# Infini-attention and a routed FFN on one core: logit maxima over two heads, the causal mask added by TensorE, four projection jobs per unit, and one emitted order for every engine

## The chip, the cores and the metric

The kernel runs on one core of one Trainium2 chip. The metric is device time in microseconds (us) of one launch; lower is better. The time of a kernel is the median over its runs. Engines: TensorE (PE; PEld is its weight load), VectorE (DVE), ScalarE (ACT), GpSimd (POOL), and SyncE (SP), which here issues all DMAs.

## The reference, cut to what matters

One sequence of S = 2048 tokens, D = 640, 32 heads of 20 channels. Attention is causal within segments of L = 512 tokens; across segments there is a linear memory `M`, `z`. Beside it stands one SwiGLU FFN for the single token with the largest router score. A sigmoid gate mixes the two.

```python
for s in range(N):                                   # N = 4 segments
    qs, ks, vs = q[:, :, s], k[:, :, s], v[:, :, s]
    logits = jnp.einsum("bhqd,bhkd->bhqk", qs, ks) * scale + mask
    a_dot = jnp.einsum("bhqk,bhkd->bhqd", _softmax(logits), vs)
    pq = phi(qs)                                     # where(t > 0, t + 1, exp(t))
    a_mem = (pq @ M) / ((pq @ z)[..., None] + 1e-6)
    outs.append(g * a_mem + (1.0 - g) * a_dot)
    pk = phi(ks)
    M = M + jnp.einsum("bhld,bhle->bhde", pk, vs)
    z = z + jnp.einsum("bhld->bhd", pk)
a = outs @ wo
...
y = (silu(x_sel @ w_gate) * (x_sel @ w_up)) @ w_down * sigmoid(r_sel)   # one token
b = x + scatter(y)
return gate * a + (1 - gate) * b
```

## The kernel before

**Number format.** Products that must be exact to float32 are made of float32r parts: a tensor is split into `hi` (an ACT copy that rounds) and `lo` (a subtraction, on POOL or DVE; L144 to L146), and a product takes three matmuls, hi hi, lo hi, hi lo.

**Units and groups.** The heads are cut into two halves of 16, the sequence into four segments; a *unit* `u` (8 of them) is one half in one segment, and a *group* `n` (32 of them, four a unit) is four heads of a unit.

**Projections** (`projections`, L407; `pair_up`, L230). In each unit five T jobs make q and k with channels on partitions (tiles of 128 channels, `TILES`), and two V jobs make v with tokens on partitions. A job runs in two halves of the PE array at once (rows 0 to 63 and 64 to 127; a *pair* is one matmul in each), 15 pairs, a drain, and 15 pairs with the halves swapped ("swap"). All jobs write the one PSUM tile `sums` (two banks), so a job can start only after the one before has been copied out: `evac_t` (L278) copies a T tile by halves with ACT and DVE (L284, L285) into the `lo` tile, casts `hi`, makes `phi` (two ACT passes, then DVE L293), and at last POOL overwrites the copy with `lo` (L298). `hi` and `lo` rows go by DMA to DRAM stacks (`place`, L252) and come back (`bring_back`, L268) as `qs` and `ks`, five buffers of each, so that one matmul of 60 rows makes all three products of a logit.

**Logits.** `a_step` (L496) makes logits with queries on partitions into PSUM `a`, five steps a group. DVE adds the mask (a bf16 tile) and takes the maximum in one instruction, per head (L507); an accumulator read follows each. `m_split` and `m_rows` turn the negative maxima into two more rows of `qs` (by DMA, L528). `b_step` (L531) makes the logits again with keys on partitions (`bt`, L537), now with the maximum subtracted by those rows; ACT takes the exponential (L539), POOL zeroes what lies above the diagonal (L543).

**Values and memory.** `pv_step` (L549) sums over keys on PE into `pv`, with 32-column tiles, and copies it to `pvs` (L558); `norm` transposes and divides; `memory_read`, `memory_write` and `keys` are the linear memory. The group's rows go to DRAM (`otok`).

**FFN** (`ffn`, L709). Routing, ten steps up (two weights, five each), an activation, eight steps down; each step loads `wt` (two buffers) and later multiplies. A step that yields 2 is one that has to wait for something.

**Output** (`out_stage`, L749). For each of 16 tiles of 128 tokens: rows of `otok` are read, transposed, split, multiplied with `wo` (30 pairs of 320 columns into `sums`), and added (L799) to `xf`, the gated residual: `x` loaded (L724) into one of the four `raw` buffers, scaled by ACT (L727), mixed by DVE with the FFN's row (L728).

**What sets the order.** PE and SP run in the order in which the code emits; ACT, DVE and POOL are ordered by the tile framework's scheduler. The emitted order is a fixed table of events per group (`plan`, L882): fractions of a group at which the steps of `a`, `b`, the maxima's rows and `full` (PV, norm and other chores, L858) stand; before each event the projections are run to `LEAD` = 3.6 groups ahead of the logits (`proj.to`). Loads and splits are tied to jobs (`prefetch`, L359). The FFN starts at n = 13 and takes one waiting step in each `full`; at n = 28 the rest of it is emitted at once, and then the output stage is started:

```python
            if n == 13 and k == 0:
                side.append(Fill(ffn()))
            if n == 28 and k == 0:
                for f in side:
                    f.finish()
                extra.append(Fill(out_stage()))
```

Of the kernel before, what the change touches and what calls it, by code (L numbers as in the profile page):

```python
# [19 lines left out]
NH = 2  # L20
# [26 lines left out]
JOBS = ("T0", "T1", "T2", "T3", "T4", "V0", "V2")  # L47
LAST = {"T1": 0, "T2": 1, "T3": 2, "T4": 3}
# [7 lines left out]
def tile_infini_mod(  # L56
# [27 lines left out]
    ctx.enter_context(tc.manual_schedule(engines={mybir.EngineType.PE, mybir.EngineType.SP}))  # L84
# [6 lines left out]
    mask = one.tile([128, L], BF16, name="mask")  # L91
    nc.vector.memset(mask, 0.0)
    nc.vector.tensor_scalar(mask[:, L - 128:], jp, 0.0, NEG, op0=OP.is_gt, op1=OP.mult)
    junk = one.tile([128, L], BF16, name="junk")
# [38 lines left out]
    W, raws = {}, {}  # L133

    def raw_tile(key, *srcs):
        t = pool.tile([128, D], F32, tag="raw", bufs=4, name="raw")
        n = 0
        for src in srcs:
            w = src.shape[-1]
            nc.sync.dma_start(t[:, n:n + w], src)  # L140
            n += w
        raws[key] = t[:, :n]

    def split(hi, lo, raw, eng):  # L144
        nc.scalar.copy(hi, raw)
        eng.tensor_tensor(out=lo, in0=raw, in1=f32(hi), op=OP.subtract)  # L146
# [6 lines left out]
    def w_tile(key):  # L153
        shape, tag, bufs = ([128, KT, VC + 2], "wv", 1) if key[0] == "V" else ([128, D], "w", KT + 1)
# [5 lines left out]
    def load_t(hf, j):  # L160

        for kind, g in READY[j]:
            t = pool.tile([128, KT, 4, DH], F32, tag="raw", bufs=4, name="raw")
            nc.sync.dma_start(t.rearrange("p k j d -> p k (j d)"), columns(kind, hf, g, GC).rearrange("(k p) m -> p k m", p=128))
            raws[kind, hf, g] = t

    def split_t(hf, j, eng=None):

        for kind, g in READY[j]:
            t = raws.pop((kind, hf, g))  # L170
            for i, tl in enumerate(TILES):
                for r0, r1, kind_, g_, c0 in tl:
                    if (kind_, g_) != (kind, g):
                        continue
                    hi, lo = W.get(("T", hf, i)) or w_tile(("T", hf, i))
                    src = t[:, :, :, c0 // 4:(c0 + r1 - r0) // 4].rearrange("p k j d -> p k d j")
                    h_, l_ = (f32(w).rearrange("p (k m) -> p k m", k=KT)[:, :, r0:r1].rearrange("p k (d j) -> p k d j", j=4)
                              for w in (hi, lo))
                    split(h_.bitcast(F32R), l_.bitcast(F32R), src, eng or nc.gpsimd)


    VPARTS = ((0, 0, 3), (0, 3, 5), (1, 0, 3), (1, 3, 5))

    def load_v(hf, i):
        qt, k0, k1 = VPARTS[i]
        w = 2 * GC + (2 if hf == 0 and qt == 0 else 0)
        t = pool.tile([128, D], F32, tag="raw", bufs=4, name="raw")[:, :(k1 - k0) * w].rearrange("p (k m) -> p k m", m=w)
        nc.sync.dma_start(t, columns("v", hf, 2 * qt, w).rearrange("(k p) m -> p k m", p=128)[:, k0:k1])
        raws["V", hf, i] = t

    def split_v(hf, i, eng=None):
        raw = raws.pop(("V", hf, i))
        qt, k0, k1 = VPARTS[i]
        w = raw.shape[2]
        hi, lo = W.get(("V", hf)) or w_tile(("V", hf))
        c = slice(162 * qt, 162 * qt + w)
        split(hi[:, k0:k1, c], lo[:, k0:k1, c], raw, eng or nc.gpsimd)

    def load_w(key):
        raw_tile(key, wo[128 * key[1]:128 * key[1] + 128, :])  # L200

    def split_w(key, eng=None):
        raw = raws.pop(key)
        hi, lo = w_tile(key)
        split(hi, lo, raw, eng or nc.gpsimd)


    X = {}

    def load_x(u, k):  # L210
        s = u % SEG
        raw_tile(("x", u, k), xT[128 * k:128 * k + 128, L * s:L * s + L])

    def split_x(u, k, eng=None):
        hi = pool.tile([128, L], F32R, tag="xhi", bufs=KT + 2, name="xhi")
        lo = pool.tile([128, L], F32R, tag="xlo", bufs=KT + 2, name="xlo")
        split(hi, lo, raws.pop(("x", u, k)), eng or nc.gpsimd)
        X[u, k] = hi, lo

    COST_MM = 1.08 / 2.4  # L220
    om = {}
    groups = [0]
    current = [0]
    chunks = [0.0]
    visits = [0]
    clock = [0]

    sums = psum.tile([128, 2, 512], F32, name="sums")

    def pair_up(o0, f0, o1, f1, cost):  # L230


        n = 3 * KT

        def mm(o, f, i, r, phase):
            return nc.tensor.matmul(o, *f(i, r), start=phase == 0 and i == 0, stop=phase == 1 and i == n - 1)  # L236

        for i in range(n):
            mm(o0, f0, i, 0, 0)
            mm(o1, f1, i, 1, 0)  # L240
            yield cost
        yield "swap"
        nc.tensor.drain()
        for i in range(n):
            mm(o1, f1, i, 0, 1)
            mm(o0, f0, i, 1, 1)
            yield cost

    aim = [0.0, 0.0]
    TOL = 0.11  # L250

    def place(kind, m, c0, hi, lo, r0, n):  # L252

        d = stk[kind][m % NS]
        first, gap, low = {"q": (0, GC, 2 * GC), "k": (0, 2 * GC, GC)}[kind]
        src = f32(hi)[r0:r0 + n, :L]
        nc.sync.dma_start(bass.AP(tensor=d.tensor, offset=d.offset + (first + c0) * L, ap=[[L, n], [gap * L, 2], [1, L]]),
                          bass.AP(tensor=src.tensor, offset=src.offset, ap=[list(src.ap[0]), [0, 2], list(src.ap[1])]))

        def low_rows():  # L260
            nc.sync.dma_start(d[low + c0:low + c0 + n, :], f32(lo)[r0:r0 + n, :L])
            if c0 + n == GC:
                backs.append((kind, m))
        lows.append(low_rows)

    lows, backs = [], []

    def bring_back():  # L268
        while backs:
            kind, m = backs.pop(0)  # L270
            assert m - NS < current[0]
            d = stk[kind][m % NS]
            dst = f32((qs if kind == "q" else ks)[m % NS])
            for b in range(2):
                nc.sync.dma_start(dst[64 * b:64 * b + ST].rearrange("r p t -> r (p t)"),
                                  d.rearrange("(r b p) t -> r b (p t)", b=2, p=2)[:, b])

    def evac_t(u, j):  # L278
        s = u % SEG
        hi = pool.tile([128, D], F32R, tag="hi", bufs=2, name="hi")  # L280
        lo = pool.tile([128, D], F32R, tag="lo", bufs=2, name="lo")
        c = f32(lo)[:, :L]
        h = L // 2
        nc.scalar.copy(c[:, :h], sums[:, 0, :h])  # L284
        nc.vector.tensor_copy(c[:, h:], sums[:, 1, :h])  # L285
        nc.scalar.copy(hi[:, :L], c)
        for r0, r1, kind, g, c0 in TILES[j]:
            place(kind, 4 * u + g, c0, hi, lo, r0, r1 - r0)
        if s < SEG - 1 or j in QGROUP:
            e = pool.tile([128, L], F32, tag="phi", bufs=3, name="phi")  # L290
            nc.scalar.activation(e, c, AF.Relu, scale=-1.0)
            nc.scalar.activation(e, e, AF.Exp, scale=-1.0)
            nc.vector.scalar_tensor_tensor(out=e, in0=c, scalar=1.0, in1=e, op0=OP.add, op1=OP.max)  # L293
            if s < SEG - 1:
                turned.append((clock[0], lambda: keys(u, j, e)))
            if s > 0 and j in QGROUP:
                chores.append((clock[0], lambda: memory_read(u, QGROUP[j], e)))
        nc.gpsimd.tensor_tensor(out=lo[:, :L], in0=c, in1=f32(hi)[:, :L], op=OP.subtract)  # L298
# [3 lines left out]
    def keys(u, j, e):  # L302
        for r in range(2):
            parts = [t for t in TILES[j] if t[2] == "k" and t[0] // 64 == r]
            if parts:
                p = slice(64 * r, 64 * r + 64)
                tp = psum.tile([128, 4, 64], F32, tag="misc", bufs=2, name="ktp")
                for c in range(4):
                    nc.tensor.transpose(tp[:, c, :], e[p, 128 * c:128 * c + 128], identf[p, p])
                for r0, r1, kind, g, c0 in parts:  # L310
                    nc.scalar.copy(kk[:, g, :, c0:c0 + r1 - r0], tp[:, :, r0 - 64 * r:r1 - 64 * r])

    def memory_read(u, g, e):
        nm = psum.tile([128, 4, GW], F32, tag="misc", bufs=2, name="nm")
# [656 lines left out]
```

## Time and profile before

| what | value |
|---|---|
| time, median of 3 runs | 879.21 us (877.89 to 883.76) |
| the profiled execution | 877.44 us |
| its span | 875.7 us |
| mean granted clock of PE | 0.89 of full speed |

The views quoted below are of that one execution. In the lists by line, a row is: line, engine, operation, output and inputs by the program's names, shape, count, then the busy time in us and the mean ns of one, then the idle time of the engine before them and what ended it. In the lists in order of time, a row is start, length (us) and what ran. In the waits, a row is who waited for whom, the total in us, how often, and the longest. Lengths of single matmuls are latencies; the rate is read from the distance of starts.

### The profile page before, as it was taken

How to read it: one execution, taken by the hardware profiler on the slowest of the kernel's cores; microseconds unless marked ns; L12 is line 12 of the kernel's file. 1: busy time of each engine (PE TensorE's matmuls, PEld its weight loads, DVE VectorE, ACT ScalarE, POOL GpSimd, SP SyncE). 2: the span in 40 equal slices, each digit the busy share in tenths (PEclk: the TensorE clock that was granted, in tenths of full speed). 3: DMA queues.
4: the chain of work that ended last, by engine and by line, in shares of the span. 5: the costliest groups of instructions: out<-in, count | busy, mean ns of one | idle time of the engine just before them, and what ended most of it. 6: DMA issues, size and time to landing. Idle time of an engine off the chain costs nothing.

```text
span 875.7 us, 19037 instructions
## 1 busy us (share of the span) xinstructions
PE 678.4 (77%) x7316; PEld 532.7 (61%) x7316; DVE 448.3 (51%) x1498; ACT 365.6 (42%) x646; POOL 257.4 (29%) x329
## 2 busy tenths in 40 slices
PE   5667887887878778878888888888874767776777
PEld 4556766666665666667766766666640345664766
DVE  5175555566455655675665566555560355422232
ACT  5333554545355545555554445444530034241110
POOL 3322233333345445243223323343340011021000
PEclk9878999999899989999999999898895679788889
DMA  4762357155525552563467256735644324133431
GB/s 125 204 210 59 97 141 202 25 140 149 145 63 147 168 155 70 169 185 80 140 190 234 80 154 183 210 105 176 192 135 130 99 91 130 54 113 92 133 93 61
DMA packets 81458, 116.67 MB, mean 133 GB/s; under 512 B 36240, under 2 KB 41880, under 8 KB 81368
## 3 DMA queue, kind: packets, MB, share of 16 engines
q1 hardware_dynamic: 81368, 115.46, 45.7%
q8 instruction: 58, 0.95, 0.5%
q14 instruction: 32, 0.26, 0.1%
HBM read 72.94 MB, written 41.96 MB: 131 GB/s over the span
## 4 chain that ended last, share of the span: by engine, by line
PE 30%; DMA 13%; DVE 12%; ACT 6%; issue 4%; SPq 3%; POOL 1%; POOLq 0%; DVEq 0%; ACTq 0%
PE sums L236 14%; DVE junk L507 6%; PE pv L555 6%; DMA xf<-in_x_dram 4%; DMA wt<-in_wd_dram 3%; DMA out_dram<-xf 3%; PE a L503 2%; PE nm L316 2%; SPq L528 2%; PE otp L575 1%; PE bt L537 1%; PE ffn L694 1%; DVE xf L799 1%; ACT p L539 1%; DMA stkk<-lo 1%
## 5 line engine op out<-in xcount | busy, mean ns | idle before, releaser
L507 DVE CUSTOM_DVE_ANT_0 junk<-a,mask 128x384 bf16<-128x384 f32 (+3 forms) x512 | 249.9, 488 | 147.3 <-PE a L503 136.6
L539 ACT ACTIVATE p<-bt 128x1024 f32<-128x1024 f32 x160 | 163.9, 1024 | 145.3 <-PE bt L537 144.5
L543 POOL TENSOR_SCALAR_AFFINE_SELECT p<-p 128x512 f32<-128x512 f32 (+1 forms) x160 | 87.3, 547 | 280.8 <-ACT p L539 271.6
L236 PE MATMUL sums<-xhi,whi 64*128 64x256 f32 x800 | 132.9, 325 | 41.5 <-DVE lo L285 26.1
L236 PE MATMUL sums<-xlo,whi 64*128 64x256 f32 x800 | 126.1, 306 | 1.2 <-POOL xlo L146 1.0
L236 PE MATMUL sums<-xhi,wlo 64*128 64x256 f32 x800 | 124.1, 303 | 0.0
L236 PEld LDWEIGHTS sums<-xhi,whi 64*128 64x128 f32 x800 | 85.6, 206 | 58.4 <-DVE lo L285 31.5
L503 PE MATMUL a<-ks,qs 60*128 60x384 f32 (+3 forms) x512 | 76.0, 347 | 45.9 <-DVE mx L507 42.0
L555 PE MATMUL pv<-p,va 128*32 128x512 f32 (+3 forms) x1024 | 84.0, 472 | 11.8 <-ACT num L318 9.9
L236 PEld LDWEIGHTS sums<-xlo,whi 64*128 64x128 f32 x800 | 86.6, 207 | 7.0 <-issue 3.7
L236 PEld LDWEIGHTS sums<-xhi,wlo 64*128 64x128 f32 x800 | 86.5, 208 | 0.5 <-issue 0.2
L503 PEld LDWEIGHTS a<-ks,qs 60*128 60x128 f32 x512 | 48.2, 203 | 57.4 <-DVE mx L507 52.3
L298 POOL TENSOR_TENSOR lo<-lo,hi 128x512 fp32r<-128x512 f32 x40 | 51.0, 1274 | 108.3 <-DVE phi L293 80.6
L236 PE MATMUL sums<-whi,oh 64*128 64x320 f32 x320 | 59.7, 361 | 29.3 <-DVE xf L799 26.7
L537 PE MATMUL bt<-qs,ks 62*128 62x384 f32 (+3 forms) x512 | 75.1, 344 | 7.7 <-ACT p L539 6.1
L236 PE MATMUL sums<-whi,xhi 64*128 64x322 f32 (+1 forms) x320 | 61.1, 369 | 13.4 <-DVE rg L352 5.5
L555 PEld LDWEIGHTS pv<-p,va 128*32 128x32 f32 x1024 | 33.9, 117 | 58.8 <-issue 37.4
L558 ACT COPY pvs<-pv 128x512 f32<-128x512 f32 x32 | 18.8, 586 | 103.6 <-PE pv L555 103.6
L236 PEld LDWEIGHTS sums<-whi,oh 64*128 64x128 f32 x320 | 35.9, 211 | 37.0 <-issue 24.3
L236 PE MATMUL sums<-whi,xlo 64*128 64x322 f32 (+1 forms) x320 | 58.0, 348 | 0.0
L537 PEld LDWEIGHTS bt<-qs,ks 62*128 62x128 f32 x512 | 49.1, 209 | 14.1 <-ACT p L539 10.8
L236 PE MATMUL sums<-wlo,xhi 64*128 64x322 f32 (+1 forms) x320 | 57.1, 343 | 0.0
(109 smaller groups left out, 1090.9 us busy)
## 6 DMA issues: line engine op xcount, KB each, us to landing
qs<-stkq SPq DMA_DIRECT2D x64, 240.0 KB
ks<-stkk SPq DMA_DIRECT2D x64, 240.0 KB
raw<-in_xT_dram SPq DMA_DIRECT2D x40, 256.0 KB
stkq<-hi SPq DMA_DIRECT2D x32, 320.0 KB
stkq<-lo SPq DMA_DIRECT2D x32, 160.0 KB
otok<-ou SPq DMA_DIRECT2D x32, 160.0 KB
xf<-in_x_dram SPq DMA_DIRECT2D x16, 320.0 KB
out_dram<-xf SPq DMA_DIRECT2D x16, 320.0 KB
```

What stands on the lines that cost most here:

```text
L236: return nc.tensor.matmul(o, *f(i, r), start=phase == 0 and i == 0, stop=phase == 1 and i == n - 1)
L298: nc.gpsimd.tensor_tensor(out=lo[:, :L], in0=c, in1=f32(hi)[:, :L], op=OP.subtract)
L316: nc.tensor.matmul(nm[:, c, :], e[:GC, 128 * c:128 * c + 128], mbd[:, g, :], start=True, stop=True)
L503: nc.tensor.matmul(a[:, b, at:at + w], q_, ks[n % NS][64 * b:64 * b + ST, p, :w], start=True, stop=True)
L507: nc.vector.tensor_tensor_reduce(out=junk[:, :w], in0=a[:, b, at:at + w], in1=mask[:, L - w:], scale=1.0, scalar=-3e38, op0=OP.add, op1=OP ...
L528: nc.sync.dma_start(f32(qs[n % NS])[64 * b + ST + r:64 * b + ST + r + 1].rearrange("r p (i t) -> r (p i) t", t=128), mr[16 * b + 8 * r:16 ...
L537: nc.tensor.matmul(bt[:, b, at:at + w], k_, qs[n % NS][64 * b:64 * b + ST + 2, p, L - w:], start=True, stop=True)
L539: nc.scalar.activation(pt, bt, AF.Exp, scale=SCALE)
L543: nc.gpsimd.affine_select(out=d, in_=d, pattern=[[0, e[1]] for e in dims[:-1]] + [[1, 128]], base=0, channel_multiplier=-1, compare_op=OP. ...
L555: nc.tensor.matmul(pv[32 * j:32 * j + 32, 128 * c:], va[u % 2][:, c, VW * h:VW * h + 32], pt_tiles[n, j % 2, c][:, j // 2], start=c == 0, ...
L558: nc.scalar.copy(pvs[n], pv)
L575: nc.tensor.transpose(tp[:, c].rearrange("p j r -> p (j r)"), o[:, 128 * c:128 * c + 128], identf)
```

## The change

Five things are done at once.

1. *Maxima.* One `tensor_reduce` takes the maxima of both heads of a step (two PSUM banks) in place of one masked maximum and one accumulator read per head.
2. *Mask on PE.* After each logit row, four more matmuls (two heads of 64 rows times two halves of the array; 128 columns) add the mask's diagonal block into PSUM: `pick` (a shifted identity) times `tri` (-1e30 above the diagonal).
3. *Four jobs per unit.* Two T jobs make two whole tiles each (512 columns in each bank); the fifth tile is cut into 128-column parts that run ahead of the V part in the other two jobs.
4. *Order by a rough clock.* `now` holds a time for each engine; every emitted piece adds an estimated duration and is marked with when its result, its PSUM buffer or its DMA will be there. The main loop emits a logit step, PV, a chore or a projection pair when that clock says it is ready. Loads stand in one list and are issued when a `raw` buffer is free; DMAs are issued when the clock passes the time of their data. `LEAD` is 3.9. FFN steps that wait run at any visit; the output stage follows the projections in the same stream, `x` is loaded two tiles at a time into the buffers of the V weights, and the mix is done one tile ahead.
5. *Emitted order on all engines:* ACT, DVE and POOL too.

Beside these, the copy of a T tile now lies in `phi` (so POOL's `lo` reads it, and DVE's `phi` step overwrites it after that), the `w` ring has one buffer less, and the fifth tile is evacuated and placed in two halves.

```diff
-    LEAD = 3.6
+LEAD = 3.9
-    ctx.enter_context(tc.manual_schedule(engines={mybir.EngineType.PE, mybir.EngineType.SP}))
+    ctx.enter_context(tc.manual_schedule())
...
+    for h in range(2):
+        for r in range(2):
+            p = slice(64 * r, 64 * r + 64)
+            off = 64.0 * (h - r)
+            nc.vector.tensor_scalar(pick[p, h], jp[p], off, None, op0=OP.is_equal)
+            nc.vector.tensor_scalar(tri[p, h], jp[p], off, NEG, op0=OP.is_gt, op1=OP.mult)
...
     def a_step(n, k):
...
         for i, p, at, w in LOGITS[k]:
             for b in range(2):
                 q_ = qs[n % NS][64 * b:64 * b + ST, p, 128 * i:128 * i + 128]
-                nc.tensor.matmul(a[:, b, at:at + w], q_, ks[n % NS][64 * b:64 * b + ST, p, :w], start=True, stop=True)
+                nc.tensor.matmul(a[:, b, at:at + w], q_, ks[n % NS][64 * b:64 * b + ST, p, :w], start=True, stop=False)
+            for h in range(2):
+                for b in range(2):
+                    r = slice(64 * b, 64 * b + 64)
+                    nc.tensor.matmul(a[:, b, at + w - 128:at + w], pick[r, h], tri[r, h], start=False, stop=h == 1)
+        end = pe(0.26 + 0.12 * len(LOGITS[k]), free["a"], stack(n))
         for i, p, at, w in LOGITS[k]:
-            w = min(w, 128 * i + 128)
-            for b in range(2):
-                nc.vector.tensor_tensor_reduce(out=junk[:, :w], in0=a[:, b, at:at + w], in1=mask[:, L - w:], scale=1.0,
-                                               scalar=-3e38, op0=OP.add, op1=OP.max,
-                                               accum_out=mx[n][:, b, p, i:i + 1])
+            nc.vector.tensor_reduce(out=mx[n][:, :, p, i:i + 1], in_=a[:, :, at:at + w], axis=AX.X, op=OP.max)
+            end = run("DVE", 0.16 + w / 480, end)
+        free["a"] = end + 0.1
...
+    now = {"PE": 0.0, "ACT": 0.0, "DVE": 0.0, "POOL": 0.0, "DMA": 0.0}
+    def run(engine, us, *ready):
+        now[engine] = max([now[engine], *(r + 0.12 for r in ready)]) + us
+        return now[engine]
...
+                if job < 2:
+                    j0 = 2 * job
+                    parts = [(sums[:, 0], channels(u, j0, 0, L), sums[:, 1], channels(u, j0 + 1, 0, L), L, lambda i: None)]
                 else:
+                    c = 2 * (job - 2)
+                    n = 128
...
+                    parts = [(sums[:, 0, :n], channels(u, 4, 128 * c, n), sums[:, 1, :n], channels(u, 4, 128 * c + n, n), n,
+                              lambda i: None),
+                             (sums[:, 1, n:n + w], tokens(u, c + 1, w), sums[:, 0, n:n + w], tokens(u, c, w), w, note)]
...
     def evac_t(u, j, src, t0, t1, scalar):
...
+        if scalar:
+            nc.scalar.copy(dst, src)
+        else:
+            nc.vector.tensor_copy(dst, src)
...
+            nc.gpsimd.tensor_tensor(out=lo, in0=c, in1=f32(hi), op=OP.subtract)
...
+                nc.vector.scalar_tensor_tensor(out=c, in0=c, scalar=1.0, in1=r, op0=OP.add, op1=OP.max)
+                end = run("DVE", 0.15 + w / 960, end, now["POOL"])
...
     def out_load(t):
-        xf[t] = pool.tile([128, D], F32, tag="raw", bufs=4, name="xf")
-        nc.sync.dma_start(xf[t], x[128 * t:128 * t + 128, :])
+        i = t // 2 % 2
+        p = pool.tile([128, KT, VC + 2], F32, tag=("wvhi", "wvlo")[i], bufs=1, name="xf").rearrange("p a b -> p (a b)")
+        p = p[:, :2 * D].rearrange("p (c e) -> p c e", c=2)
+        nc.sync.dma_start(p, x[128 * t:128 * t + 256, :].rearrange("(c p) e -> p c e", p=128))
...
+    while True:
+        t = now["PE"]
+        flush_dmas(t)
+        if feed() or piece():
+            continue
...
+        if pv and (where[0] == "open" or blocked or gt > 1e8 or left[0] > 2.0):
+            logits(0.2, t)
+            visit(0.7 if where[0] == "mid" else 1.3, True)
+            continue
+        if old and where[0] == "swap":
+            logits(0.2, t)
+            visit(3.0, False)
+            step()
+            continue
+        if logits(0.0, t):
+            continue
+        if gt <= t:
+            step()
+            continue
...
+        now["PE"] = min(times)
```

More of the change, by code (lines that the diff above doesn't have):

```diff
@@ L924, in tile_infini_mod, with step, gate_at @@
-    full(NG - 1)
-    extra[0].run(3000)
-    while chores:
-        chores.pop(0)[1]()
-    stores()
-    visits[0] += 1
-    extra[0].finish()
+    side = []
+    fill = both()
+    filling = [True]
+    def step():
+        try:
+            next(fill)
+        except StopIteration:
+            filling[0] = False
+            where[0] = "end"
+    def gate_at():
+        if not filling[0] or over[0] < 4 * NU and done_b[0] + NS + 1 < chunks[0]:
+            return 1e9
+        if where[0] == "wait":
+            return 1e9
+        return sums_free[0] if where[0] == "open" else 0.0
```

916 lines of the change are left out of this document (511 added, 405 removed).

## The prediction

> **What bounds the kernel now.** I read the page first, then the span cut at the `pv` copies (L558) of groups 0, 26 and 27, then the instructions in order of time, the groups by shape, the waits, and the chain that ended last.
>
> ```profile
> span 875.7 us, 19037 instructions
> PE 678.4 (77%) x7316; PEld 532.7 (61%) x7316; DVE 448.3 (51%) x1498; ACT 365.6 (42%) x646; POOL 257.4 (29%) x329
> ```
> ```profile
> 0.00:96.80 96.80, 65.00 (x662) 55.62 (x664) 47.97 (x135) 38.12 (x74) 29.43 (x36) 0.86 0.51 144
> 96.80:637.80 541.00, 446.68 (x5104) 352.26 (x5108) 314.71 (x1137) 271.85 (x480) 203.85 (x258) 0.92 0.51 145
> 637.80:698.20 60.40, 37.55 (x242) 17.62 (x236) 19.61 (x53) 8.16 (x13) 8.68 (x12) 0.69 0.42 120
> 698.20:875.70 177.50, 129.16 (x1316) 107.16 (x1316) 66.03 (x175) 47.45 (x80) 15.46 (x24) 0.87 0.31 95
> ```
> ```profile
> 96.80:637.80 541.00, 18.46 (x104) 11.81 (x104) 15.26 (x27) 0.92 0.51 145
> ```
>
> The columns of the windows are stretch, length, busy PE, PEld, DVE, ACT, POOL (the last one for `pvs` only: PE, PEld, ACT), granted clock, DMA share, GB/s. There are four stages: the start until group 0 is through PV (97 us); the steady stage, 27 copies, so 26 groups at 541/26 = 20.8 us; one group that takes 60.4 us; and the tail of 177.5 us (groups 28 to 31 and the output rows). In the steady stage PE is busy 446.68 of 541 us (83%, 17.2 us a group), while DVE, ACT and POOL have 58, 50 and 38%. PE is the nearest bound, but 17% of it is holes, and its clock is not full. Holes and clock go together:
>
> ```profile
> 200.00:250.00 50.00, 39.48 (x428) 30.55 (x428) 28.80 (x105) 24.48 (x45) 18.89 (x24) 0.90 0.41 118
> 400.00:450.00 50.00, 43.08 (x539) 33.62 (x536) 31.84 (x121) 24.79 (x42) 16.81 (x22) 1.00 0.44 122
> ```
>
> With PE busy 79% of a stretch the granted clock is 0.90, with 86% it is 1.00. The long group is the FFN's down part, run to its end at n = 28 (L920): a load of `wt` and then its matmuls, in turn. The tail is a chain through DMA for most output tiles:
>
> ```profile
> 686.07 3.02 DMA wt<-in_wd_dram
> ...
> 689.13 1.28 PE ffn L694 x4
> ...
> 835.58 2.35 DMA out_dram<-xf
> ...
> 837.95 4.88 DMA xf<-in_x_dram
> ...
> 842.94 0.84 ACT xf L727
> ...
> 843.80 0.89 DVE xf L728
> 844.69 0.93 DVE xf L799 x2
> ...
> 854.23 2.46 PE sums L236 x30
> ...
> 859.27 1.02 DVE xf L799 x2
> ...
> 860.43 1.58 PE sums L236 x18
> ```
>
> Store, load, mix, add: 835.58 to the next store near 845.6, 10 us a tile. Two tiles later, with loads that no longer wait, the period is 860.43 - 854.23 = 6.2 us.
>
> **The change, PE's work.** Rates come from starts in full-clock stretches:
>
> ```profile
> 407.83 0.31 PE L236 MATMUL sums<-whi,xhi 64*128 64x320 f32 x2
> 407.98 0.31 PE L236 MATMUL sums<-wlo,xhi 64*128 64x320 f32 x2
> ...
> 415.73 0.28 PE L236 MATMUL sums<-xlo,whi 64*128 64x256 f32 x2
> 415.85 0.40 PE L503 MATMUL a<-ks,qs 60*128 60x384 f32 x4
> 416.09 0.33 PE L236 MATMUL sums<-xhi,whi 64*128 64x256 f32 x2
> ```
> ```profile
> 508.38 0.39 PE L537 MATMUL bt<-qs,ks 62*128 62x512 f32 x2
> 508.61 0.28 PE L236 MATMUL sums<-xlo,whi 64*128 64x256 f32 x2
> ```
>
> A pair (two halves of the array at once) costs 0.15 us at 320 columns, 0.12 at 256, 0.23 at 512; a pair of 384 and one of 128 cost 0.24 together. By 0.15/320 x 384 = 0.18 the 128-column pair costs 0.06.
>
> Four jobs for seven: five T jobs of 30 pairs at 0.12 are 18.0 us a unit; two of 30 pairs at 0.23 and two parts of 30 at 0.06 are 17.4. V is as before. So 0.6 us a unit, 0.15 a group: nothing. What counts is that `sums` is handed over four times a unit and not seven.
>
> The mask on PE: after each of the 8 logit rows of a group come two heads x two halves of the array of `pick` times `tri`, 128 columns, that is 16 pairs. From below 16 x 0.05 = 0.8 us (320-column rate), from above 16 x 0.12 = 1.9 us, were a weight load not hidden behind so short a stream (the 256 rate is the least seen for a pair with its loads in a row). I take 0.06, the row with 128 columns: 1.0 us a group, 31 us in all. It lies on PE, the bound, and is a true loss.
>
> **The change, DVE.** Times of one maximum before, and nearest rows for the new one:
>
> ```profile
> L507 DVE CUSTOM_DVE_ANT_0 junk<-a,mask 128x512 bf16<-128x512 f32 x128 | 88.1, 688 | 55.5 <-PE a L503 53.4
> L507 DVE CUSTOM_DVE_ANT_0 junk<-a,mask 128x384 bf16<-128x384 f32 x128 | 71.1, 555 | 43.6 <-PE a L503 41.6
> L507 DVE DVE_READ_ACCUMULATOR2_ANT mx<- 128x1 f32 x512 | 42.2, 82 | 0.0
> L507 DVE CUSTOM_DVE_ANT_0 junk<-a,mask 128x256 bf16<-128x256 f32 x128 | 54.2, 424 | 44.9 <-PE a L503 41.6
> L507 DVE CUSTOM_DVE_ANT_0 junk<-a,mask 128x128 bf16<-128x128 f32 x128 | 36.5, 285 | 3.4
> ```
>
> Before: 88.1 + 71.1 + 54.2 + 36.5 + 42.2 = 292 us, 9.1 a group. A step from 256 to 512 elements costs 264 ns, so 1.03 ns an element; 1024 elements in one reduce cost 688 + 512 x 1.03 = 1.22 us in place of 2 x (688 + 82) = 1.54. The four widths, each 2w elements, give 1.22 + 0.95 + 0.69 + 0.42 = 3.3, twice a group 6.6: DVE gets 2.5 us a group back, 81 us in all (none at worst, if a reduce costs as much as its two predecessors). The Trainium skill (VectorE: DVE Perf Modes, Rules for kernel authors) speaks against this op: expect `tensor_reduce` at the lowest rate, think of restructuring. At the rate that its table gives, one element a cycle at 0.96 GHz, the 1024 elements would take 1.07 us and a fixed part, an estimate; the custom operation's 1.03 ns an element shows the same rate, so nothing is lost by the change of op. The gain is off the bound: it is worth the hole it shortens.
>
> ```profile
> PE a L503 <- DVE mx L507: 26.0, 30, 2.2
> ```
>
> That is 26 us over 500 us of the steady stage, 1 us a group: about what the mask adds.
>
> **The order.** The rest is the order. Every engine's instructions now stand in the order in which a clock model emitted them; PE takes a logit step, PV, a transpose only when the model says that its inputs are there, else another projection pair. ACT's copies of an evacuation are given out one by one when ACT is nearly free. I can bound what this does, not derive it. Busy PE at the present clock is 17.2 + 1.0/0.92 - 0.15 = 18.1 us a group. By the two 50-us rows, with holes of 6 to 8% the clock would be about 0.96 or better, so 18.1 x 0.92/0.96 = 17.4; at 94% busy (a guess between the best stretch, 86%, and none idle) 18.5 us a group, against 20.8.
>
> FFN: it starts at about the same group, but its waiting steps (22 of them: 4 routing, 10 up, 8 down) can run at each PV and at each middle of a job with chores, not once a group; over the 15 groups that are left this suffices if 1.5 of them run per group. I take 5 us left of the 60.4 - 20.8 = 40; the ends are 0 and 40.
>
> Tail: loads of `x` come in pairs, two tiles ahead, into the freed V weights; the mix runs in the tile before; the store goes out at once. The 10-us cycle falls and 6.2 us is next, up to 7.2 where the transposes stand in the middle of the products and no longer in the hole: 16 x 6.7 = 107. The last four groups have no projections beside them: five steps of logits for `a` and five for `bt` at 0.24, the mask 1.0, and PV:
>
> ```profile
> 504.90 2.36 PE L555 MATMUL pv<-p,va 128*32 128x512 f32 x32
> 507.05 0.94 PE L666 MATMUL ffn<-wt,xs 128*32 128x432 f32 x8
> ```
>
> PV takes 2.15 by its starts; with norm and reads at about 1.5 (a guess) that is 7 us each, 8 with holes, 31 together. Sum 138 us, ends 125 and 160.
>
> Start: the first job now needs four weight blocks and not two, but is longer; LEAD goes from 3.6 to 3.9 groups; loads are no longer tied to jobs. I take 92 us, ends 85 and 100. Places of tile 4 in halves add four DMA issues a unit on SP; the DMA share of 0.51 covers them.
>
> Sum: 92 + 27 x 18.5 + 5 + 138 = 734.5 us of span, against 875.7. The profiled execution took 877.44 us, 1.7 over its span, and the median is 879.21, 1.8 over that: **738 us**.
>
> **Rivals.** *Clock stays at 0.92.* The Trainium skill (TensorE: Matmul & The Clock Gate, Why this matters for your kernels) has the clock fall only after idle gaps of over some 3 us. The longest of the waits just quoted is 2.2 us and the clock is 0.92 in that stage, so the trace does not follow that rule. If small holes are not what lowers it, then closing them does not raise it: 18.1/0.94 = 19.3 a group, 27 x 0.8 = 22 us more, 760.
>
> *Holes stay.* The model knows one clock, and one latency per DMA; where it is off, PE waits in a fixed order as before. At 83% busy a group takes 18.1/0.826 = 21.9: 95 + 27 x 21.9 + 10 + 140 + 3.5 = 840. For it: the old order was also laid by hand and holds at 83%. Against: four hand-overs for seven, and a shorter maximum. Within 1% would need the stall or the tail to stay as well.
>
> *Slower: DVE behind POOL.* Before, `lo` and the copy share a tile, so POOL waits for DVE:
>
> ```profile
> POOL lo L298 <- DVE phi L293: 80.6, 30, 10.1
> ```
> ```profile
> L298 POOL TENSOR_TENSOR lo<-lo,hi 128x512 fp32r<-128x512 f32 x40 | 51.0, 1274 | 108.3 <-DVE phi L293 80.6 <-issue 10.4 <-DVE mx L507 5.2
> L146 POOL TENSOR_TENSOR xlo<-raw,xhi 128x512 fp32r<-128x512 f32 x37 | 47.6, 1292 | 31.8 <-ACT xhi L145 28.4 <-DMA stkq<-hi 3.3
> ```
>
> Now the copy lies in `phi`, and DVE's `phi` step waits until POOL has read it. POOL may have an `xlo` (1.3 us) and selects before its `lo` (1.3 us); behind the waiting DVE instruction stand, in order, the maxima and the next evacuation of `sums`, for which PE waits. 46 such steps; at 3.5 us each, all of it seen by PE, 161 us: 900. It decides from 3.2 us. Against it: `lo` is emitted before `phi`, two ACT passes lie between, POOL is 38% busy.
>
> **The numbers.** First case (738) 0.47, clock stays (760) 0.19, holes stay (840) 0.21, within 1% (about what a measurement can tell from no change) 0.05, slower 0.08. Faster by over 1% is 0.47 + 0.19 + 0.21 = 0.87. The first case alone runs from 680 (97% busy at full clock: 18.1 x 0.92/0.97 = 17.2 a group, start 85, FFN 0, tail 125) to 803 (start, FFN and tail at their upper ends). The range goes up to the third case, 845; left out are the slow ends, 0.13, and a little below.
>
> **What would show it.** Right: no stretch of `wt` loads and `ffn` in turn; PE over 90% busy and a clock over 0.95 between PV copies some 18.5 us apart; `mx` reduces of 1.2 us at w = 512; output tiles 6 to 7 us apart with no `xf` load in the chain; PE groups `a<-tri,pick` near 31 us of stream. Wrong: DVE `phi` waiting for POOL `lo` by tens of us; `sums` waiting for its copies as long as now; 128-column pairs at 0.12 us.

## The result, and the profile after

| | time, us | ratio to before, 95% interval |
|---|---|---|
| before, 4 runs | 878.55 (867.77 to 883.76) | |
| after, 4 runs | 788.98 (783.72 to 798.93) | 0.8997 (0.8876 to 0.9118) |

The change makes the kernel 10% faster; 16% was forecast. Single executions of one kernel can be over 1.5% slower than its fastest (798.93 beside 783.72 us of after): the times are medians of all executions, the ratios leave such ones out. The profiled execution took 790.6 us. Its page, top lines:

```profile
span 788.9 us, 19342 instructions
## 1 busy us (share of the span) xinstructions
PE 698.2 (88%) x7860; PEld 576.9 (73%) x7860; DVE 406.1 (51%) x730; ACT 366.0 (46%) x646; POOL 267.4 (34%) x343
```

Its span, cut at the same places (the `pvs` copies, now L708, of groups 0, 26 and 27), and last one stretch of 15 us, all with the columns of the prediction's windows:

```profile
0.00:87.20 87.20, 64.78 (x618) 53.73 (x620) 45.09 (x65) 37.48 (x72) 36.10 (x42) 0.90 0.60 168
87.20:621.10 533.90, 494.81 (x5628) 407.24 (x5628) 284.62 (x521) 270.81 (x478) 209.09 (x266) 0.93 0.54 152
621.10:639.10 18.00, 17.78 (x252) 14.69 (x244) 9.27 (x17) 8.26 (x15) 5.82 (x8) 1.00 0.43 119
639.10:788.90 149.80, 120.80 (x1374) 101.26 (x1374) 67.17 (x127) 49.41 (x83) 16.40 (x27) 0.95 0.40 126
268.00:283.00 15.00, 14.25 (x110) 13.67 (x112) 5.80 (x16) 5.39 (x11) 9.22 (x11) 0.54 0.45 119
```

Of the 87 us of span, the start gives 9.6, the 26 groups only 7.1 (20.8 to 20.5 us a group), the group in which the FFN stalled 42.4, the tail 27.7. In the 26 groups PE is busy 494.81 of 533.90 us, 93% where it was 83%: the holes did close (94 us before, 39 after), but 48 us of busy time took their place. Why PE has more to do is seen in the list of PE's instructions in order of time, on a logits step at full clock:

```profile
208.42 0.34 PE L622 MATMUL a<-ks,qs 60*128 60x384 f32 x2
208.60 0.34 PE L626 MATMUL a<-tri,pick 64*128 64x128 f32 x4
208.77 0.28 PE L622 MATMUL a<-ks,qs 60*128 60x128 f32 x2
208.88 0.39 PE L626 MATMUL a<-tri,pick 64*128 64x128 f32 x4
209.11 0.36 PE L359 MATMUL sums<-whi,xhi 64*128 64x322 f32 x2
```

From 208.42 to 209.11 are 0.69 us; without the mask's eight matmuls such a step took 0.24 (the row of 415.85 in the prediction). In the cut fifth tile, pairs of 128 columns follow each other at 0.11 us. In the next view (same list, other place) they stand at 268.28, 268.39 and 268.50, and after 269, where the granted clock is half, 0.22 apart:

```profile
268.28 0.28 PE L359 MATMUL sums<-xhi,wlo 64*128 64x128 f32 x2
268.39 0.27 PE L359 MATMUL sums<-xlo,whi 64*128 64x128 f32 x2
268.50 0.28 PE L359 MATMUL sums<-xhi,whi 64*128 64x128 f32 x2
...
269.54 0.42 PE L359 MATMUL sums<-xlo,whi 64*128 64x128 f32 x2
269.76 0.42 PE L359 MATMUL sums<-xhi,whi 64*128 64x128 f32 x2
```

The new maxima, by shape, cost what the sum said (1.22, 0.95, 0.69, 0.42 us); the other row is the weight load of the mask:

```profile
L629 DVE TENSOR_REDUCE mx<-a 128x2 f32<-128x1024 f32 x64 | 78.3, 1224 | 59.6 <-PE a L626 58.4 <-PE mtp L656 1.1
L629 DVE TENSOR_REDUCE mx<-a 128x2 f32<-128x768 f32 x64 | 61.3, 957 | 83.5 <-PE a L626 83.2
L629 DVE TENSOR_REDUCE mx<-a 128x2 f32<-128x512 f32 x64 | 41.2, 686 | 33.9 <-PE a L626 33.6
L629 DVE TENSOR_REDUCE mx<-a 128x2 f32<-128x256 f32 x64 | 26.6, 416 | 0.0
L626 PEld LDWEIGHTS a<-tri,pick 64*128 64x128 f32 x1024 | 100.7, 201 | 3.6
```

Waits of the span that bear on the steps; the first row is of the kernel before, where PE waited for the copies of `sums`, and the second is the same wait in after (the copy now lies in `phi`):

```profile
PE sums L236 <- DVE lo L285: 30.2, 31, 3.7
...
PE sums L359 <- DVE phi L420: 4.9, 7, 1.4
PE a L622 <- DVE mx L629: 13.3, 9, 7.3
PE sums L359 <- DVE xf L981: 8.3, 11, 1.2
DVE kk L876 <- DMA y<-yrow: 7.2, 1, 7.2
DVE phi L446 <- POOL lo L429: 6.3, 2, 4.0
```

One stall is the price of a strict order: DVE waits 7.2 us for the FFN's row, the maxima stand behind that instruction, and PE's logits behind them (7.3 us, the longest wait of the row `a` for `mx`). The chain that ended last has both, one after the other:

```profile
638.90 4.99 DMA y<-yrow
...
643.98 0.83 DVE kk L876
...
645.40 1.21 DVE mx L629 x2
...
646.74 0.58 PE a L622 x2
```

### The profile page after: what moved, and what is told of

It is laid out like the page before. It is cut to its first block, busy times and chain, and to the rows that moved or that the text cites. A ratio compares the mean times of both kernels' runs of the same rounds, so it can differ in the third digit from the quotient of the medians.

```text
span 788.9 us, 19342 instructions
## 1 busy us (share of the span) xinstructions
PE 698.2 (88%) x7860; PEld 576.9 (73%) x7860; DVE 406.1 (51%) x730; ACT 366.0 (46%) x646; POOL 267.4 (34%) x343
## 4 chain that ended last, share of the span: by engine, by line
PE 75%; DMA 9%; DVE 7%; issue 3%; ACT 3%; SPq 1%; POOL 0%; DVEq 0%; ACTq 0%; POOLq 0%
PE sums L359 41%; PE pv L702 8%; PE a L622 5%; PE a L626 5%; PE bt L677 5%; DMA qs<-mr 3%; PE nm L475 3%; PE otp L729 3%; DVE mx L629 2%; PE mp L498 2%; PE ttp L918 1%; DVE xf L981 1%; DMA stkq<-lo 1%; ACT p L681 1%; DMA ks<-stkk 1%
## 5 line engine op out<-in xcount | busy, mean ns | idle before, releaser
L629 DVE TENSOR_REDUCE mx<-a 128x2 f32<-128x1024 f32 (+3 forms) x256 | 202.0, 821 | 177.0 <-PE a L626 175.1
L359 PE MATMUL sums<-xhi,whi 64*128 64x128 f32 (+1 forms) x640 | 131.8, 371 | 20.9 <-ACT xhi L164 12.2
L359 PE MATMUL sums<-xhi,wlo 64*128 64x128 f32 (+1 forms) x640 | 129.1, 359 | 3.1 <-DVE wlo L167 3.1
L359 PE MATMUL sums<-xlo,whi 64*128 64x128 f32 (+1 forms) x640 | 129.7, 361 | 0.0
L622 PE MATMUL a<-ks,qs 60*128 60x384 f32 (+3 forms) x512 | 100.4, 361 | 22.8 <-DVE mx L629 13.3
L626 PEld LDWEIGHTS a<-tri,pick 64*128 64x128 f32 x1024 | 100.7, 201 | 3.6
L626 PE MATMUL a<-tri,pick 64*128 64x128 f32 x1024 | 97.4, 264 | 0.0
L622 PEld LDWEIGHTS a<-ks,qs 60*128 60x128 f32 x512 | 59.5, 199 | 37.3 <-issue 21.3
L702 PE MATMUL pv<-p,va 128*32 128x512 f32 (+3 forms) x1024 | 75.5, 435 | 0.4 <-ACT mr L658 0.4
L429 POOL TENSOR_TENSOR lo<-phi,hi 128x512 fp32r<-128x512 f32 (+1 forms) x48 | 53.1, 1107 | 46.7 <-ACT hi L425 30.4
L702 PEld LDWEIGHTS pv<-p,va 128*32 128x32 f32 x1024 | 30.2, 109 | 43.4 <-issue 35.3
```

The source lines that it names most:

```text
L359: nc.tensor.matmul(o, a, b, start=phase == 0 and i == 0, stop=phase == 1 and i == n - 1)
L429: nc.gpsimd.tensor_tensor(out=lo, in0=c, in1=f32(hi), op=OP.subtract)
L622: nc.tensor.matmul(a[:, b, at:at + w], q_, ks[n % NS][64 * b:64 * b + ST, p, :w], start=True, stop=False)
L626: nc.tensor.matmul(a[:, b, at + w - 128:at + w], pick[r, h], tri[r, h], start=False, stop=h == 1)
L629: nc.vector.tensor_reduce(out=mx[n][:, :, p, i:i + 1], in_=a[:, :, at:at + w], axis=AX.X, op=OP.max)
L702: nc.tensor.matmul(pv[32 * j:32 * j + 32, 128 * c:], va[u % 2][:, c, VW * h:VW * h + 32], pt_tiles[n, j % 2, c][:, j // 2], start=c == 0, ...
```

## The experiments

Each kernel was timed in three rounds against the kernel before on the same chip. The stages of the profiled spans, cut as above (us; "group" is the mean of the 26):

| kernel | time, us | ratio (95%) | start | group | 27th group | tail |
|---|---|---|---|---|---|---|
| before | 878.55 | | 96.8 | 20.8 | 60.4 | 177.5 |
| after | 788.98 | 0.900 (0.888 to 0.912) | 87.2 | 20.5 | 18.0 | 149.8 |
| 1 five jobs | 790.66 | 0.898 (0.891 to 0.905) | 84.5 | 20.6 | 23.6 | 146.3 |
| 2 mask in bf16 | 784.98 | 0.894 (0.887 to 0.902) | 90.6 | 20.2 | 17.5 | 150.3 |
| 3 no mask | 744.72 | 0.847 (0.838 to 0.857) | 92.3 | 18.1 | 28.2 | 149.5 |
| 4 mask on DVE | 785.95 | 0.896 (0.888 to 0.903) | 90.0 | 20.6 | 27.5 | 129.0 |
| 5 three engines free | 863.24 | 0.980 (0.971 to 0.989) | 89.9 | 22.2 | 18.0 | 179.4 |
| 6 higher prices | 814.74 | 0.929 (0.921 to 0.938) | 89.8 | 21.1 | 28.7 | 147.3 |
| 7 before, FFN steps | 849.46 | 0.968 (0.958 to 0.978) | 94.0 | 21.3 | 18.0 | 178.3 |
| 8 before, all emitted | 878.79 | 1.009 (1.005 to 1.012) | 102.1 | 22.0 | 62.9 | 141.5 |
| 9 no mask, same order | 777.08 | 0.887 (0.882 to 0.892) | 87.3 | 20.1 | 15.9 | 149.3 |
| 10 no mask, five jobs | 727.98 | 0.831 (0.828 to 0.835) | 81.8 | 18.2 | 23.6 | 148.1 |
| 11 before, new maxima | 897.05 | 1.021 (1.014 to 1.028) | 95.6 | 21.3 | 65.0 | 180.1 |
| 12 mask on DVE, same order | 785.76 (774, 783, 788, 794) | none | 86.5 | 20.2 | 16.1 | 152.3 |

**1. Five jobs.** The fifth tile is a job of its own, 30 pairs of 256 columns.

```diff
-        share = [2 * 2 * L, 2 * 2 * L, L + 4 * VC, L + 4 * VC]
+        share = [2 * 2 * L, 2 * 2 * L, 2 * L, 4 * VC, 4 * VC]
+                elif job == 2:
+                    n = L // 2
+                    parts = [(sums[:, 0, :n], channels(u, 4, 0, n), sums[:, 1, :n], channels(u, 4, n, n), n, lambda i: None)]
```

> The fifth tile gets a job of its own with 30 pairs of 256 columns, in place of two parts of 30 pairs of 128; nothing else of the change is touched. Theory of the size (a pair of 128 columns takes 0.11 us in a row, not 0.06): PE's stream falls by 60 x 0.112 - 30 x 0.12 = 3.1 us a unit, 25 us in all, against one more hand-over of sums per unit, about 1 us each; 789 falls to 765 to 780. Rival (PE's time is not what counts, the waits of the fixed order are): 785 to 800, by the hand-over alone.

```profile
84.50:619.90 535.40, 474.12 (x5229) 380.18 (x5227) 279.71 (x513) 267.60 (x461) 210.44 (x261) 0.93 0.54 155
```

In its 26 groups PE is busy 20.7 us less, 0.8 a group, so the cut tile costs what the pairs of 0.11 us say; the time is the same, because the holes grew by as much (39 to 61 us). So PE's stream fell as the theory of the size said, but its 765 to 780 us did not come; the time is that of the rival.

**2. Mask in bf16.** `pick` and `tri` in the smaller type.

```diff
-    pick = one.tile([128, 2, 128], F32R, name="pick")
-    tri = one.tile([128, 2, 128], F32R, name="tri")
+    pick = one.tile([128, 2, 128], BF16, name="pick")
+    tri = one.tile([128, 2, 128], BF16, name="tri")
```

> pick and tri become bf16 tiles, so that the mask's weights are 2 bytes wide; the number of matmuls stays. If the weight load sets the 0.11 us of a mask pair and is quicker for 2-byte weights, 16 x 0.05 x 32 = 26 us of PE go and the time falls to 760 to 770. If the pair keeps its 0.11 us, 789 within 1%.

By shape, the mask's weight load takes half as long:

```profile
L626 PEld LDWEIGHTS <-pick 64*128 64x128 bf16 x1024 | 37.2, 100 | 24.0 <-issue 15.9
```

A step of 12 matmuls falls from 0.69 to 0.52 us, one of six from 0.41 to 0.33. So a pair of 128 columns in a row is not bound by its stream of columns alone, which at the rate of the 320-column pairs takes 0.06 us. The weight load is the likely term, since its record halves; but the edit makes the streamed `tri` two bytes wide as well, and no run separates the two. The 0.65 us a group (3 x 0.17 + 2 x 0.08), 21 us in all, hardly reach the time: 4 us less, with overlapping intervals, where 760 to 770 us were expected.

**3, 9 and 10. No mask.** The mask's matmuls are left out, so that the maxima go over unmasked logits and are only a larger shift, which the softmax divides out; POOL still zeroes what lies above the diagonal.

```diff
-                nc.tensor.matmul(a[:, b, at:at + w], q_, ks[n % NS][64 * b:64 * b + ST, p, :w], start=True, stop=False)
-            for h in range(2):
-                for b in range(2):
-                    r = slice(64 * b, 64 * b + 64)
-                    nc.tensor.matmul(a[:, b, at + w - 128:at + w], pick[r, h], tri[r, h], start=False, stop=h == 1)
-        end = pe(0.26 + 0.12 * len(LOGITS[k]), free["a"], stack(n))
+                nc.tensor.matmul(a[:, b, at:at + w], q_, ks[n % NS][64 * b:64 * b + ST, p, :w], start=True, stop=True)
+        end = pe(0.26, free["a"], stack(n))
```

> The mask matmuls are left out, and the maxima are taken over unmasked logits (a larger shift, which the softmax divides out again); the reduce over two heads stays. PE's stream falls by 1024 matmuls in 512 pairs, 16 a group at 0.06 to 0.11 us, 31 to 57 us in all. If PE's stream is what the steady stage waits for: 789 falls to 735 to 760, a group from 20.5 to 18.5 to 19.5 us. If the steady stage is held by waits of the fixed order (as the five jobs and the mask on DVE, which took as much from PE and gave 786 to 791, seem to say): 780 to 795, with the holes of PE grown by what its stream lost.

Kernel 9 leaves the last line as it was, so that the clock still counts the mask and the order is that of after. Kernel 10 is kernel 3 with the five jobs.

> The mask matmuls are left out as in the run without a mask, but the clock model still counts them, so that every other instruction stands where it stood in the changed kernel. A logit step of 12 matmuls takes 0.69 us from start to the next work, one of 4 takes 0.24, one of 6 0.41 against 0.23: 2 x 0.17 + 3 x 0.45 = 1.7 us a group, 54 us in all. If the time lost to the mask is PE's stream itself: 735 to 750, as without a mask. If the run without a mask owed its 745 to the other order: 770 to 789.

> No mask matmuls (and none in the clock), and the fifth tile in a job of its own. With PE relieved of the mask, the 25 us of the 128-column pairs against one more hand-over a unit are weighed again: if PE's stream is still what counts, 725 to 738; if hand-overs cost what the pairs save, 745 within 1%, as the five jobs alone did.

The 26 groups of kernel 3, then those of kernel 9 with a stretch of it:

```profile
92.30:563.80 471.50, 433.95 (x4732) 337.62 (x4736) 278.50 (x517) 268.38 (x474) 206.79 (x264) 0.95 0.59 168
```
```profile
87.30:610.40 523.10, 473.94 (x4792) 374.99 (x4796) 284.63 (x521) 269.64 (x477) 209.73 (x266) 0.89 0.54 155
...
108.00:125.00 17.00, 16.25 (x120) 15.17 (x122) 7.34 (x17) 5.14 (x12) 5.31 (x6) 0.51 0.30 80
```

Without the mask and with the order that the clock then makes, the groups take 18.1 us and the kernel 44 us less. With the same matmuls in the order of after, only 12 us come: PE's clock falls to 0.89. All runs agree in this: over the whole span the mean clock is 0.927 to 0.945 in the four runs of kernel 3 and 0.897 to 0.905 in those of kernel 9. In the 26 groups half clock holds for 44 us of kernel 3 and 119 of kernel 9; if PE takes twice as long there, that is some 37 of the 52 us by which kernel 9 is longer, and its holes (49 us against 38) are 12 more. The best version is kernel 10: both costs of short streams gone, 17% under the kernel before.

**4 and 12. Mask back on DVE.** The masked maximum of before, in the new stream; kernel 4 has the clock's prices to match, kernel 12 the prices and so the order of after.

```diff
-            nc.vector.tensor_reduce(out=mx[n][:, :, p, i:i + 1], in_=a[:, :, at:at + w], axis=AX.X, op=OP.max)
+            w = min(w, 128 * i + 128)
+            for b in range(2):
+                nc.vector.tensor_tensor_reduce(out=junk[:, :w], in0=a[:, b, at:at + w], in1=mask[:, L - w:], scale=1.0,
+                                               scalar=-3e38, op0=OP.add, op1=OP.max,
+                                               accum_out=mx[n][:, b, p, i:i + 1])
```

> The maxima of before return (one masked maximum per head on DVE, no mask matmuls), in the new order, with the clock model's times set to match. Theory of the size: PE loses 16 x 0.112 = 1.8 us a group, 57 us in all, DVE gains 2.5 us a group but was busy 53% of the steady stage; the time falls to 735 to 760, so the mask on PE was a loss by itself. Rival (the shorter maximum is what made the new order possible, PE waits for it): 790 to 830, with PE waiting for mx by over 40 us.

> The mask is back on DVE with one masked maximum per head (2.5 us a group more on DVE, no mask on PE), while the clock model still counts the changed kernel's prices, so the order stays the changed kernel's. Beside the run without a mask in the same order, only DVE's operation differs. If DVE's length is hidden: equal to that run, 735 to 750. If the maxima are on the path of the logits: 30 to 50 us more, 775 to 795.

Both medians lie some 3 us below that of after, less than the spread of the runs. The longer maxima do lengthen a wait; the waits of kernel 12 have

```profile
PE a L618 <- DVE mx L624: 30.2, 23, 8.6
```

where after has 13.3 us and kernel 9 has 14.3. But kernel 9, with the short maxima, the same order and no mask on PE either, takes 777 us, and the four runs of kernel 12 lie on both sides of that; the profiled spans are 775.6 and 780.9 us. So DVE's length is nearly hidden in this order, and it is not the maxima that take back what PE saves. In kernel 4 PE waits for them for only 6.1 us. In the 26 groups of kernels 4, 9 and 12 PE is busy 19 to 21 us less than in after, while the holes grow by 20, 10 and 13 us and the clock is 0.91, 0.89 and 0.90 where after has 0.93. By these times the first two parts of the change are worth nothing in the new order.

**11. Before with the new maxima and the mask on PE** (the edit of `a_step` in the diff, without the clock).

> The kernel before with the first two parts of the change alone: one reduce over two heads, the mask on PE; order, jobs and FFN as before. If the shorter maximum (2.5 us a group of DVE) is worth as much as the mask's 1.7 us of PE: 879 within 1.5%. If in the old order the maximum was a wait of PE (26 us in 500): 850 to 865. If the mask's PE time is all that counts: 900 to 935.

In the old order these parts alone cost 20 us (876.59 for before in the same rounds), which lies between the cases. PE waits for the maxima for 18.0 us in place of 42.0, but in the 26 groups it is busy 28 us longer.

**5. Three engines free.** PE and SP stand in the order of after, ACT, DVE and POOL are left to the framework.

```diff
-    ctx.enter_context(tc.manual_schedule())
+    ctx.enter_context(tc.manual_schedule(engines={mybir.EngineType.PE, mybir.EngineType.SP}))
```

> Only PE and SP keep the emitted order; ACT, DVE and POOL are again ordered by the framework's scheduler, as before the change. If the emitted order on these engines carries a part of the gain: over 800. If it costs (engines stuck behind a waiting instruction, the slower rival of the prediction): under 780. If neither: 789 within 1%.

**8. Before, all emitted:** the opposite edit, in the kernel before.

> The kernel before with ACT, DVE and POOL in its own emitted order, and nothing else. In the new kernel the emitted order of these three was worth 863 - 789 = 74 us. If that gain belongs to the three engines' order by itself: 879 falls by 40 to 80 here too. If it needs an order written for all engines (the old code emits long runs of ACT and DVE work at one place, behind which exponentials and maxima wait): no gain or a loss, 880 to 960.

The two need each other: of the 90 us, 74 go when the three engines are set free (44 in the 26 groups, 30 in the tail), yet the same line in the kernel before gains nothing: its tail is 36 us shorter, its 26 groups 31 us longer. The stages of kernel 5 (26 groups, tail) and a wait that has doubled:

```profile
89.90:668.00 578.10, 517.34 (x5626) 425.46 (x5622) 284.74 (x522) 270.51 (x478) 210.37 (x265) 0.89 0.49 140
686.00:865.40 179.40, 131.75 (x1374) 111.36 (x1374) 64.18 (x126) 48.89 (x80) 16.23 (x26) 0.87 0.34 105
```
```profile
PE a L622 <- DVE mx L629: 25.6, 19, 4.1
```

The tail is the surprise. It is 179 us in kernel 5, which has the new loads of `x`, and 141.5 in kernel 8, which has the old ones. In kernel 5 the chain goes through a store and a load of `x` again (831.10, 2.16 us, then 833.32, 4.00 us). The chain of kernel 8 runs through products and additions alone, 6.2 us a tile:

```profile
828.53 2.48 PE sums L236 x30
...
831.03 1.02 DVE xf L799 x2
...
832.19 2.46 PE sums L236 x30
...
834.73 2.48 PE sums L236 x30
```

**7. Before, FFN steps.** A waiting FFN step runs at a second place in each group. The FFN's row then lands in a buffer that a late memory write has still to read, so the memory behind the last groups is changed; no instruction is left out.

```diff
-                if f.last != 2:
+                if f.last == 2 and k == 3:
+                    f.debt = 0.0
+                    f.run(1.0)
+                elif f.last != 2:
```

> The kernel before with one edit: a waiting FFN step may also run at the fourth logit step of each group, so that they run twice a group and none is left at n = 28. By the prediction the long group of 60.4 us falls to about 21 and no other stage changes by more than the FFN steps' own 1 us each: 879 falls by 30 to 40, to 839 to 849. Rival (the steps' loads delay the stacks and rows of the steady stage, and give it back): over 860.

The 27th group falls from 60.4 to 18.0 us, the others rise by 0.5 us each: 27 us less than the kernel before in the same rounds (876.01), where 30 to 40 were expected.

**6. Higher prices in the clock.** The model's matmul times put at what the trace shows for short streams.

```diff
-        return (cols * 1.04 + 16) / 2400
+        return max(cols * 1.04 + 16, 269) / 2400
...
-        end = pe(0.26 + 0.12 * len(LOGITS[k]), free["a"], stack(n))
+        end = pe(0.26 + 0.22 * len(LOGITS[k]), free["a"], stack(n))
```

> Only the clock model is changed: a pair of 128 columns counts 0.112 us and a logit row's mask 0.22 us, as measured, where it counted 0.062 and 0.12; the instructions are the same, their order is another. If the wrong price in the model is what makes PE meet its inputs late or early: 765 to 780. If not: 789 within 1%, the cost of the pairs being in their number.

Neither case came: the order that follows is 26 us slower than that of after, with the same instructions: 14 us of it in the 26 groups (548.0 for 533.9), 11 in the 27th. Why closer prices make a worse order stays open.

## Why the prediction was right, and where it was wrong

**Right: sign, FFN, the DVE times, the rivals.** The FFN's stall is gone (18.0 us for that group, 23.5 forecast; the 7.3 us behind the FFN's row come at the start of the tail in their place), and kernel 7 shows that more places for its waiting steps do it alone. The holes of the steady stage closed to 7% (6% forecast), so "holes stay" is not the case, and PE's wait for the copies of `sums` fell from 30.2 to 4.9 us. DVE `phi` waited for POOL `lo` twice, 6.3 us in all; the slower rival needed 3.2 us at each of 46 steps. But the sign did not come from the stage that the forecast was mainly about: of the 60 us that it gave the 26 groups 7 came, and of the 87 us of the span the FFN's group and the tail gave 70, the tail for another cause than the one named. The FFN carries the sign by a mechanism that was rightly forecast; that the tail came out near its size is luck.

**Wrong: the size of the 128-column pair.** I took 0.06 us, from one pair that stood alone after a 384-column one, and put 0.12 at the upper end. In a row they take 0.11, near the 0.12 that the forecast itself had named as a sign of being wrong. The lone pair's weights had been loaded under the longer stream ahead of it: the four loads of that step ran from 415.73 to 416.04, under the pairs of 256 and 384 columns that start at 415.73 and 415.85. The mask so costs 2 x 0.17 + 3 x 0.45 = 1.7 us a group where I had 1.0, and the cut tile 60 x 0.11 = 6.7 us a unit against 30 x 0.12 = 3.6 for whole pairs, 0.8 a group lost where I had 0.15 gained. Together that is some 1.6 us more a group. PE's busy time is 494.81/26 = 19.0 where the forecast had 17.4, but not all of that difference is stream: at full clock the two are 19.0 x 0.93 = 17.7 and 17.4 x 0.96 = 16.7, so 1.0 us is more work and 0.6 the lower clock. The other terms of the forecast were thus some 0.6 us too large, and which of them is not shown. Kernel 1 measured the cut tile by itself, kernel 9 the mask. The Trainium skill (TensorE: Matmul & The Clock Gate, LDWEIGHTS) gives the load of a weight as its columns over 1.2 GHz, by which 128 columns take 107 ns, an estimate. The trace agrees only in part: pairs in float32r stand 0.11 us apart, but the record of one load is 201 ns, and with bf16 in kernel 2 the pairs stand 0.07 us apart.

**Wrong as a rule: "holes and clock go together".** The forecast took a clock of 0.96 from closed holes; it is 0.93 with 93% busy, which is nearer the rival in which the clock stays (0.92). The two rows of 50 us were too few. Two others of the kernel before are

```profile
250.00:300.00 50.00, 39.88 (x486) 32.83 (x486) 27.17 (x100) 27.50 (x46) 24.50 (x32) 0.95 0.52 138
...
550.00:600.00 50.00, 43.90 (x514) 34.82 (x506) 27.25 (x98) 25.11 (x43) 20.19 (x25) 0.93 0.51 150
```

so 80% busy stands beside a clock of 0.95 and 88% beside 0.93. The sum of the holes does not set the clock: in the 26 groups kernel 11 has 14% holes at 0.95, kernel 9 has 9% at 0.89.

What matters is where the holes lie and how short the matmuls behind them are. The records of the clock change in steps of 3.4 us. Over the 26 groups of all fourteen traces, PE is busy 52% (mean) of a step ahead of a fall to half clock, and 91% of the steps at full clock after which it stays full. Ahead of the fall at 269.2 in after PE stands idle for 0.50 and 0.65 us. Then, at half clock, take the steps in which PE is busy 95% or more, and add up the columns of the matmuls that start in them (both halves of the array): 7300 (mean) where full clock comes next, 4100 where half clock stays. There are 10 steps of the second kind in after (268 to 283 with pairs of 128 columns, transposes and 84-column memory reads is such a place) and 16 in kernel 9; one in kernel 1, where the cut tile has pairs of 256 columns, one each in kernels 3 and 10, and none in before and kernels 7, 8 and 11, which have no cut tile. So in these traces half clock begins behind holes that fall close together and lasts while the matmuls are short. This is a count over the records and not an experiment: kernel 1 has fewer such steps than after but more falls (15 for 9), and the same clock. The Trainium skill (TensorE: Matmul & The Clock Gate, Why this matters for your kernels) advises against idle gaps of over some 3 us, since a window of idle brings half clock; the longest gap that PE's list shows from 255 to 284 us in after is 0.65 us, so the trace does not follow that rule.

**Right in size, wrong in cause: the tail.** The chain through store and load is gone and the last tiles follow each other at 6.2 to 7.5 us, as the step said. But I credited the loads of `x` in pairs: kernel 5 has them and a tail of 179 us, kernel 8 has not and 141.5. It is the emitted order on ACT, DVE and POOL. Why after has 149.8 and not the 138 forecast is in part seen: between additions the chain has also transposes (PE `ttp`, 7.7% of the last 110 us), and the stall of 7 us behind the FFN's row falls into the start of the tail. Kernel 4, with the mask on DVE and another order of all engines, has 129.0; why is not shown.

By stages, in us of span: start 87.2 against 92 forecast, 26 groups and the 27th 551.9 against 27 x 18.5 + 5 = 504.5, tail 149.8 against 138. The middle term is nearly the whole miss of 54.4. Its stream was mis-sized and its clock was too high, but the two do not simply come back: with the cut tile whole (kernel 1) the time is the same, and without the mask the groups take 20.1 us in the order of after and 18.1 in the order that then follows.

**What is not settled.** The share of one part cannot be read from taking it away: shorter streams come out as holes (1), as holes and a lower clock (4, 9, 12), and in one case in full (3). Orders of the same instructions lie 26 to 32 us apart (after and 6; 3 and 9), more than what most parts of the change are worth. So "parts 3 to 5 together" is as far as the 90 us can be given to anything but the FFN (27, from kernel 7) and the emitted order within the new stream (74, from kernel 5), which overlap. One wait can be given more closely: that for the copies of `sums`, 30.2 us before, is 32.6 in kernel 8 and 7.9 in kernel 5, so it left with parts 3 and 4 and not with part 5.

## What to carry to other kernels

Price a short matmul from a row of like ones, each with its own weights, never from one that stands behind a longer stream; here halving the columns from 256 to 128 took a pair from 0.12 to 0.11 us, so cutting a tile in two nearly doubled its cost. Work that is moved to the bound engine must pay there: here the mask left a DVE at 58% for a PE at 83%, and leaving it out gained 44 us with an order of its own, though only 12 in the order of after. Judge a clock by where the holes lie and by what runs behind them, not by their sum. An emission order and the order of the other in-order engines are one thing: test them together, since each alone gave little or nothing.

## What the runs showed of the hardware

A weight load of a 64-row tile of 128 columns takes 201 ns by its records in float32r and 100 ns in bf16, at pairs 0.11 and 0.07 us apart. The granted clock fell to half for stretches of 14 and 17 us in which PE was busy 95% (after, 268 to 283, clock 0.54; kernel 9, 108 to 125, clock 0.51). Ahead of both falls stand 3.4 us with holes (after, 265.8 to 269.2, PE busy 2.32 us; kernel 9, 105.0 to 108.4, 1.75 us).
